# Loading x on the sync queue behind a large weight load, in a decode block on one core

## The chip, the cores and the metric

The kernel runs on one core of one Trainium2 chip. The metric is the device time of one execution in microseconds (us). An execution of one kernel that is over 1.5% above the fastest of the same kernel counts as slow. Times inside a trace are counted from the start of the profiled span, which is some 2 us shorter than the device time.

The engines named below are PE (TensorE, matrix multiplies), DVE (VectorE), ACT (ScalarE) and SP (SyncE, which here does nothing but issue loads). SPq and ACTq are the instruction streams in which SP and ACT issue DMAs (data transfers). The profile counts the work of the core's 16 DMA engines.

## The reference, cut to what matters

One transformer block in decode form: 4 sequences, one token each. A layernorm of x, a projection to 32 query heads, attention over the last 2048 positions of a cache with 4 key/value heads, an output projection with a residual, a second layernorm, and a gated MLP with a residual.

```python
h  = x + attention(layernorm(x) @ wq, k_cache[-2048:], v_cache[-2048:]) @ wo
h2 = h + (silu(layernorm(h) @ w1) * (layernorm(h) @ w3)) @ w2
# x: 4 x 1 x 1024 bf16 (8 KB)     wq: 1024 x 4096 (8 MB)    k, v windows: 8 MB each
# wo: 4096 x 1024 (8 MB)          w1, w3, w2: 7 MB each
```

With four rows of x there is little arithmetic per byte: about 55.6 MB have to be read once. That is the work.

## The kernel before

All large loads go through one on-chip buffer (in SBUF), `ring`, and one queue, the sync queue. A later load reuses the place of an earlier one, so its issue waits until the engines have read what lay there. `load_next(n)` issues the next n entries of a fixed plan.

```python
plan = [
    ("wq", load_rows, (0,         wq_v, N_Q, 0, 4)),     # first half of wq, 4 MB, one DMA
    ("wq", load_rows, (32 * KIB,  wq_v, N_Q, 4, 4)),     # second half, 4 MB, one DMA
    ("k",  load_kv,   (64 * KIB,  A_k_cache, 0)),        # two DMAs of 2 MB
    ("k",  load_kv,   (96 * KIB,  A_k_cache, 2)),        # two DMAs of 2 MB
    ("v",  load_kv,   (128 * KIB, A_v_cache, 0)),
    ("v",  load_kv,   (0,         A_v_cache, 2)),        # takes the place of wq's first half
    ("wo", load_rows, (32 * KIB,  wo_v, D, 0, 32)),
    ("w1", load_rows, (96 * KIB,  w1_v, N_F, 0, 8)),     # takes the place of k and v: waits for OT_ps
    ("w3", ...), ("w3", ...), ("w2", ...), ...           # cut
]

x_sb = act.tile([B, D], BF16)
nc.scalar.dma_start(out=x_sb[:], in_=x_flat)             # x for the layernorm, ScalarE's queue
load_next(5)
# ... cut: ident, eps_t ...
x_q = act.tile([P, CG], BF16)
nc.vector.memset(x_q[:], 0.0)
for j in range(JG):                                      # x again, in the layout of the residual
    nc.scalar.dma_start(out=x_q[QD*j : QD*(j+1) : RS, :], in_=x_flat[:, j*CG : (j+1)*CG])
# ... cut: bn_stats(x_sb), rstd (Sqrt on ScalarE), xn, 8 transposes -> xnT ...
for kc in range(KC):                                     # KC = 8; kc 0..3 read wq's first half
    for hf in range(2):
        for g in range(JG):
            nc.tensor.matmul(q_ps[...], lhsT=xnT[:, kc, :], rhs=loaded["wq"][kc][...], ...)
    if kc == RQ - 1:
        load_next()                                      # second pair of v
# ... cut: q_sb, qt_ps; then 256 transposes of k (kt_ps), scores, softmax, OT_ps = p @ v, y, MLP
```

`x_sb` is needed first of all: without it there is no layernorm and no q. `x_q` is needed only at the residual, at 88 us.

Of the kernel before, what the change touches and what calls it, by code (L numbers as in the profile page):

```python
# [10 lines left out]
P = 128  # L11
# [3 lines left out]
BF16 = mybir.dt.bfloat16  # L15
# [4 lines left out]
def kernel(  # L20
# [13 lines left out]
    nc = tc.nc  # L34
# [14 lines left out]
    x_flat = A_x.flatten_outer_dims()  # L49
# [11 lines left out]
    act = ctx.enter_context(tc.tile_pool(name="act", bufs=1))  # L61
# [3 lines left out]
    JG = 4  # L65
    QD = P // JG
    RS = QD // B
    CQ = Hq * Dh // JG
    CG = D // JG
# [59 lines left out]
    def load_next(n=1):  # L129
        for _ in range(n):  # L130
            if cursor[0] < len(plan):
                kind, f, args = plan[cursor[0]]
                loaded.setdefault(kind, []).extend(f(*args))
                cursor[0] += 1

    x_sb = act.tile([B, D], BF16)
    nc.scalar.dma_start(out=x_sb[:], in_=x_flat)
    load_next(5)

    ident = const.tile([P, P], BF16)  # L140
    make_identity(nc, ident[:])
    eps_t = const.tile([P, 1], FP32)
    nc.vector.memset(eps_t[:], eps)

    x_q = act.tile([P, CG], BF16)
    nc.vector.memset(x_q[:], 0.0)
    for j in range(JG):
        nc.scalar.dma_start(
            out=x_q[QD * j : QD * (j + 1) : RS, :], in_=x_flat[:, j * CG : (j + 1) * CG]
        )  # L150

    psA_cm = tc.tile_pool(name="psA", bufs=1, space=bass.MemoryType.PSUM)
    psA = psA_cm.__enter__()
# [3 lines left out]
    for c in range(2):  # L157
# [8 lines left out]
        out=xn[:], in0=x_sb[:], scalar1=mv[:, 0:1], scalar2=rstd[:, 0:1],  # L166
# [4 lines left out]
    for kc in range(KC):  # L171
# [15 lines left out]
        out=perm[:].rearrange("p (h dq) -> p h dq", dq=JG),  # L187
        in_=ident[:].rearrange("p (dq h) -> p h dq", dq=JG),
# [12 lines left out]
    for j in range(2, JG):  # L201
        nc.vector.tensor_tensor(
            out=same[:, 0, :], in0=same[:, 0, :], in1=ident[:, j * QD : (j + 1) * QD], op=ALU.add
# [24 lines left out]
    for r in range(REP):  # L228
        nc.tensor.transpose(out=qt_ps[:, r, :], in_=q_sb[:, r * Dh : (r + 1) * Dh], identity=ident[:])
    nc.vector.tensor_copy(  # L230
        out=qz[:, :, : Hkv * QD].rearrange("p b (g z) -> p b g z", g=Hkv)[:, :, :, :REP],
        in_=qt_ps[:].rearrange("p r (g x) -> p x g r", g=Hkv)[:, :B, :, :],
# [24 lines left out]
    for u, (b, n) in enumerate(units):  # L257
        k_v = loaded["k"][b]
        kT = ktpool.tile([P, NJ, P], BF16, tag="kT")
        for t in range(NJ // TB):  # L260
            kt_ps = psA.tile([P, TB, P], BF16, tag=f"kt{nt % 4}")
            for jj in range(TB):
                nc.tensor.transpose(  # L263
                    out=kt_ps[:, jj, :], in_=k_v[:, n * NJ + t * TB + jj, :], identity=ident[:]
# [21 lines left out]
        out=Pm[:], in_=scores_ps[:], func=ACT.Exp, bias=nmax[:], scale=1.0, accum_out=rsum[:]  # L286
# [6 lines left out]
    for c in range(NSB):  # L293
# [4 lines left out]
        for g in range(Hkv):  # L298
            if g % 2 == 0:
                nc.vector.tensor_scalar(  # L300
                    out=z[:, :, g, :], in0=pt_ps[:], scalar1=mask[:, g : g + 1], scalar2=None, op0=ALU.mult
# [10 lines left out]
        out=Dm[:], in0=ident[:].rearrange("p (g b r) -> p b g r", g=Hkv, b=B),  # L312
# [38 lines left out]
    for i in range(IO):  # L351
# [34 lines left out]
        out=hn[:], in0=h1[:], scalar1=tot[:, 0:1], scalar2=rstd2[:, 0:1],  # L386
# [5 lines left out]
        out=hnT[:].rearrange("p k x -> p (k x)"), in_=hn[:].rearrange("q (c k) -> q k c", k=KC)  # L392
# [5 lines left out]
    def gate_up(kind, out_ps):  # L398
# [27 lines left out]
        out=hgT[:].rearrange("p i x -> p (i x)"),  # L426
        in_=hg[:].rearrange("q s c -> q (s c)").rearrange("q (c i) -> q i c", i=IF),
# [47 lines left out]
```

## Time and profile before

| | before |
|---|---|
| device time, median of 3 runs | 138.13 us (138.09 to 138.20) |
| bytes moved, mean rate over the span | 55.75 MB, 409 GB/s |
| layernorm starts (first BN_STATS) | 2.52 us |
| first q matmul (needs wq's first half) | 13.05 us |
| second half of the q matmuls (needs wq's second half) | 22.55 us |
| first K transpose | 27.45 us |
| w1's issue on the sync queue (needs OT_ps) | 73.22 us |

From the page of the kernel before: the span, the busy time of the engines, and the DMA row. Each digit of the row is the mean busy share of the 16 DMA engines, in tenths, in one fortieth of the span.

```profile
span 136.3 us, 2302 instructions
...
PE 67.9 (50%) x1035; PEld 42.9 (31%) x1035; DVE 42.6 (31%) x73; ACT 31.0 (23%) x36; POOL 1.7 (1%) x8
...
DMA  5999899999999999997988989989799999989960
```

The DMA engines are busy from the second slice to the last but one. PE, the busiest other engine, works half the time.

The chain of work that ended last, in order of time, for the kernel before (start, length in us, and what the time was spent on):

```profile
1.16 21.35 DMA ring<-in_A_wq_dram
...
22.55 3.18 PE q_ps L215 x32
...
73.22 25.79 DMA ring<-in_B_w_dram
...
101.59 31.37 DMA ring<-in_B_w_dram
```

The two long pieces at the end are waits for loads of the MLP weights. The one of 31.37 us is the last piece of w2, issued at 101.5 us behind transfers that were still queued. A chain that ends in such waits says that the load stream sets the end. The pieces in between (q, and the work on k that is left out here) are on the chain only because w1's issue waits for their results.

The timeline of the kernel before, first 32 us (start, length, engine, line, operation; in brackets the idle time before it and what ended it):

```profile
0.73 0.85 SPq L93 DMA_DIRECT2D ring<-in_A_wq_dram  x2
0.73 0.57 ACTq L137 DMA_DIRECT2D x_sb<-in_A_x_dram  x1
...
1.36 2.55 ACTq L148 DMA_DIRECT2D x_q<-in_A_x_dram  x4
...
2.52 1.27 DVE L158 BATCH_NORM_STATS2 stats<-x_sb 4x6 f32<-4x512 bf16 x2
...
3.94 1.28 ACT L162 ACT_TABLE_LOAD   x1 [3.94 <-DVE stats L158]
...
13.05 3.58 PE L215 MATMUL q_ps<-ring,xnT 128*4 128x512 bf16 x32 [6.05 <-DMA ring<-in_A_wq_dram]
...
22.55 3.15 PE L215 MATMUL q_ps<-ring,xnT 128*4 128x512 bf16 x32 [5.92 <-DMA ring<-in_A_wq_dram]
...
27.45 2.03 PE L263 MATMUL kt_ps<-ident,ring 128*128 128x128 bf16 x33
```

Three things to read here. ScalarE's table load (1.28 us, for the square root) starts only at 3.94 us, because the four x_q issues stand in front of it. The layernorm is ready long before PE can use it: the first q matmul waits 6.05 us more, for wq. And between the two halves of q, PE waits again for wq.

### The profile page before, as it was taken

Reading aid. Unit: us, or ns where it says so; the run is one execution under the profiler, and the core shown is the slowest. Engines: PE = TensorE matmul, PEld = TensorE weight load, DVE = VectorE, ACT = ScalarE, POOL = GpSimd, SP = SyncE. Lnnn points to the kernel's source line nnn. Section 1 sums busy time; section 2 is a strip of 40 time slices with the busy share of each in tenths; the row PEclk is TensorE's granted clock in tenths of the full one; section 3 lists DMA queues with packets and bytes.
Section 4 is the critical chain, followed back from the end, with each engine's and each line's share of the span. In section 5 each row is a group of like instructions: output and inputs, shape, how many; then the busy total and the mean of one; then the engine's idle time right before and its main releaser. Section 6 shows DMA issues by size and latency. Waiting matters only on the chain.

```text
span 136.3 us, 2302 instructions
## 1 busy us (share of the span) xinstructions
PE 67.9 (50%) x1035; PEld 42.9 (31%) x1035; DVE 42.6 (31%) x73; ACT 31.0 (23%) x36; POOL 1.7 (1%) x8
## 2 busy tenths in 40 slices
PE   0101803698989889105259538830096440900960
PEld 0100201274656565001149427610043210300840
DVE  6440000244444444609940030160000695070000
ACT  0400000155555646092944000000003300000001
POOL 5000000000000000000000000000000000000000
PEclk9999999999999999965555865897557777555577
DMA  5999899999999999997988989989799999989960
GB/s 156 462 462 443 385 413 418 423 447 423 428 437 409 437 437 423 435 582 341 538 385 365 524 365 442 459 353 522 328 412 463 434 437 447 429 388 409 426 261 5
DMA packets 2662, 55.75 MB, mean 409 GB/s; under 512 B 312, under 2 KB 344, under 8 KB 604
## 3 DMA queue, kind: packets, MB, share of 16 engines
q1 hardware_dynamic: 2592, 55.58, 95.3%
q8 instruction: 8, 0.13, 0.3%
q10 hardware_dynamic: 60, 0.02, 0.1%
q14 instruction: 2, 0.02, 0.0%
HBM read 55.59 MB, written 0.01 MB: 408 GB/s over the span
## 4 chain that ended last, share of the span: by engine, by line
DMA 58%; PE 21%; ACT 13%; DVE 5%; issue 1%; SPq 0%; ACTq 0%
DMA ring<-in_B_w_dram 42%; DMA ring<-in_A_wq_dram 16%; PE kt_ps L263 9%; ACT kT L269 6%; PE scores_ps L248 5%; ACT z L304 3%; PE q_ps L215 2%; PE g_ps L403 2%; DVE rmax L280 2%; ACT Pm L285 2%; PE OT_ps L326 2%; DVE pT L294 1%; DVE z L300 1%; ACT L285 1%; DVE q_sb L225 1%
## 5 line engine op out<-in xcount | busy, mean ns | idle before, releaser
L269 ACT COPY kT<-kt_ps 128x1024 bf16<-128x1024 bf16 x16 | 15.8, 1014 | 12.0 <-PE kt_ps L263 12.0
L263 PE MATMUL kt_ps<-ident,ring 128*128 128x128 bf16 x256 | 16.4, 219 | 0.0
L263 PEld LDWEIGHTS <-ring 128*128 128x128 bf16 x256 | 14.3, 98 | 5.0 <-issue 4.9
L267 DVE COPY kT<-kt_ps 128x1024 bf16<-128x1024 bf16 x16 | 11.1, 691 | 15.2 <-PE kt_ps L263 15.2
L215 PE MATMUL q_ps<-ring,xnT 128*4 128x512 bf16 x64 | 6.7, 596 | 12.0 <-DMA ring<-in_A_wq_dram 12.0
L403 PEld LDWEIGHTS <-hnT 128*32 128x32 bf16 x128 | 5.3, 137 | 23.1 <-issue 20.5
L248 PE MATMUL scores_ps<-kT,qz 128*32 128x512 bf16 x64 | 9.9, 609 | 3.1 <-ACT kT L269 3.1
L326 PE MATMUL OT_ps<-z,ring 128*128 128x32 bf16 x256 | 7.4, 185 | 6.7 <-ACT z L304 5.0
L403 PE MATMUL u_ps<-ring,hnT 128*32 128x448 bf16 x64 | 6.3, 572 | 8.3 <-DMA ring<-in_B_w_dram 8.3
L403 PE MATMUL g_ps<-ring,hnT 128*32 128x448 bf16 x64 | 5.4, 525 | 9.0 <-DMA ring<-in_B_w_dram 9.0
L433 PE MATMUL y_ps<-ring,hgT 128*32 128x256 bf16 x112 | 5.7, 370 | 8.4 <-DMA ring<-in_B_w_dram 8.3
L326 PEld LDWEIGHTS <-ring 128*128 128x128 bf16 x256 | 7.3, 103 | 7.4 <-issue 7.4
L433 PEld LDWEIGHTS <-hgT 128*32 128x32 bf16 x112 | 4.4, 129 | 10.3 <-issue 6.1
L215 PEld LDWEIGHTS <-xnT 128*4 128x4 bf16 x64 | 2.1, 116 | 16.2 <-issue 15.9
L353 PE MATMUL y_ps<-ring,o 128*32 128x256 bf16 x128 | 5.8, 365 | 2.0 <-DMA ring<-in_A_wo_dram 2.0
L443 ACT CAST res<-y_ps 128x256 bf16<-128x256 f32 x1 | 0.4, 372 | 26.5 <-PE y_ps L433 26.5
L304 ACT ACTIVATE z<-pt_ps,mask 128x512 bf16<-128x512 f32 x8 | 5.3, 687 | 3.5 <-DVE z L300 3.5
L225 DVE TENSOR_SCALAR q_sb<-q_ps 128x512 bf16<-128x512 f32 x1 | 0.7, 690 | 17.2 <-PE q_ps L215 17.2
L353 PEld LDWEIGHTS <-o 128*32 128x32 bf16 x128 | 4.8, 130 | 3.8 <-issue 3.1
L300 DVE TENSOR_SCALAR z<-pt_ps,mask 128x512 bf16<-128x512 f32 x8 | 5.5, 740 | 1.2 <-ACT z L304 0.8
L296 PE MATMUL pt_ps<-pT,perm 128*128 128x512 bf16 x4 | 2.4, 607 | 6.8 <-DVE pT L294 6.8
L417 DVE RECIPROCAL eg<-eg 128x896 f32<-128x896 f32 x1 | 5.8, 5753 | 0.0
(73 smaller groups left out, 40.5 us busy)
## 6 DMA issues: line engine op xcount, KB each, us to landing
ring<-in_A_wq_dram SPq DMA_DIRECT2D x2, 4096.0 KB, 16.8
ring<-in_A_k_cache_dram SPq DMA_DIRECT2D x4, 2048.0 KB, 25.5
ring<-in_A_v_cache_dram SPq DMA_DIRECT2D x4, 2048.0 KB, 40.2
ring<-in_B_w_dram SPq DMA_DIRECT2D x1, 7168.0 KB
ring<-in_B_w_dram SPq DMA_DIRECT2D x2, 3584.0 KB, 28.6
ring<-in_B_w_dram SPq DMA_DIRECT2D x1, 4352.0 KB
ring<-in_B_w_dram SPq DMA_DIRECT2D x1, 1792.0 KB
ring<-in_B_w_dram SPq DMA_DIRECT2D x1, 768.0 KB
```

What stands on the lines that cost most here:

```text
L215: nc.tensor.matmul(q_ps[QD * g : QD * g + B, hf * 512 : (hf + 1) * 512], lhsT=xnT[:, kc, :], rhs=wq_t[:, c0 : c0 + 512], start=(kc == 0), ...
L248: nc.tensor.matmul(scores_ps[QD * g : QD * (g + 1), n * 512 : (n + 1) * 512], lhsT=qz[:, b, g * QD : (g + 1) * QD], rhs=kT_v[:, g, :, :], ...
L263: nc.tensor.transpose(out=kt_ps[:, jj, :], in_=k_v[:, n * NJ + t * TB + jj, :], identity=ident[:])
L267: nc.vector.tensor_copy(out=kT[:, t * TB : (t + 1) * TB, :], in_=kt_ps[:])
L269: nc.scalar.copy(out=kT[:, t * TB : (t + 1) * TB, :], in_=kt_ps[:])
L300: nc.vector.tensor_scalar(out=z[:, :, g, :], in0=pt_ps[:], scalar1=mask[:, g : g + 1], scalar2=None, op0=ALU.mult)
L304: nc.scalar.mul(out=z[:, :, g, :], in_=pt_ps[:], mul=mask[:, g : g + 1])
L326: nc.tensor.matmul(OT_ps[:, b, :], lhsT=loaded["v"][b][:, j, :], rhs=PTz[j // NJ][:, (j % NJ) * B + b, :, :], start=(j == 0), stop=(j == J ...
L353: nc.tensor.matmul(y_ps[QD * j : QD * (j + 1), :], lhsT=o4[:, i, :, :].rearrange("p b s -> p (b s)"), rhs=loaded["wo"][i][:, j * CG : (j + ...
L403: nc.tensor.matmul(out_ps[QD * j : QD * (j + 1), hf, :HF], lhsT=hnT[:, k, :], rhs=loaded[kind][k][:, c0 : c0 + HF], start=(k == 0), stop=( ...
L417: nc.vector.reciprocal(out=eg[:], in_=eg[:])
L433: nc.tensor.matmul(y2_ps[QD * j : QD * (j + 1), :], lhsT=hgT[:, i, :], rhs=loaded["w2"][i][:, j * CG : (j + 1) * CG], start=False, stop=(i ...
```

## The change

The intent was to take all loads of x off ScalarE's queue. `x_sb` goes on the sync queue behind wq's first half, `x_q` behind its second half.

```diff
     x_sb = act.tile([B, D], BF16)
-    nc.scalar.dma_start(out=x_sb[:], in_=x_flat)
-    load_next(5)
+    x_q = act.tile([P, CG], BF16)
+    nc.vector.memset(x_q[:], 0.0)
+    load_next()
+    nc.sync.dma_start(out=x_sb[:], in_=x_flat)
+    load_next()
+    for j in range(JG):
+        nc.sync.dma_start(
+            out=x_q[QD * j : QD * (j + 1) : RS, :], in_=x_flat[:, j * CG : (j + 1) * CG]
+        )
+    load_next(3)
 
     ident = const.tile([P, P], BF16)
 ...
-    x_q = act.tile([P, CG], BF16)
-    nc.vector.memset(x_q[:], 0.0)
-    for j in range(JG):
-        nc.scalar.dma_start(
-            out=x_q[QD * j : QD * (j + 1) : RS, :], in_=x_flat[:, j * CG : (j + 1) * CG]
-        )
```

## The prediction

> **What bounds the kernel now.** The load stream. The page gives 55.75 MB at a mean 409 GB/s; the DMA row of the 40 slices is near 9 from the second slice to the last but one. The chain that ended last is 58% DMA; its last long link is a 31.4 us DMA wait (101.6 to 133.0 us) on w2, issued behind transfers still queued. PE is 50% busy, DVE 31%, ACT 23%. So a change counts only if it (a) starves the stream, (b) adds engine time to it, or (c) delays compute so far that a buffer release reaches the sync queue late.
>
> **What the change moves.** Bytes and arithmetic stay. x (5 small loads, 16 KB together) leaves ScalarE's queue; x_sb goes behind wq's first 4 MB on the sync queue, x_q behind its second.
>
> 1. x_sb lands with wq's first half, not at about 2.2 us. The Trainium skill, "DMA: Bandwidth & Descriptors", section "Queues, rings and completion order", says that an engine consumes a ring's descriptors in order and alternates between rings packet by packet; no run shows it here yet. In the timeline the first BN_STATS starts at 2.52 us and the first q matmul, which waits for wq's first half, at 13.05. I expect BN_STATS at 12.6 to 13.3 us.
>
> 2. The layernorm chain is exposed behind that landing. In the timeline, BN_STATS to first q matmul weights took 4.74 us, of which about 1.1 us was ScalarE's table load (1.28 us), held up by the four x_q issues (2.55 us) before it. Those leave ScalarE, so the table loads early. Chain: about 3.6 us; first q matmul at about 16.6 us.
>
> 3. The first 32 q matmuls take 3.58 us: done at about 20.2 us. The second half of wq is usable only at 22.55 us. About 2.3 us of slack remain, so q_ps, q_sb and the first K transposes (27.54 us) stay put. The 3.5 us delay is paid inside a wait.
>
> 4. Sync queue: five more issues at about 0.6 us each, 3 us, while wq's 8 MB keep the engines busy until 22 us. Completion semaphores shift with the order of issue: the instruction orders show that the second k load now waits for wq's first half (before: for x_sb), the fourth for wq's second half. At about 22.5 us, 6 MB of k, some 14 us of stream, are still queued, so nothing starves. The v and wo loads wait for the same things as before; w1's issue at 73.2 us hangs on OT_ps.
>
> 5. Engine time of x is the same tiny packets on another queue.
>
> **On the critical path:** nothing, by this count.
>
> **Predicted time:** 138.1 us (138.13 before), range 137.6 to 138.8. Chances: faster by over 2% 0.01, within 2% 0.97, slower by over 2% 0.02.
>
> **What the profile would show.** Right: BN_STATS at about 13 us, ScalarE's table load within the first 3 us, first q matmul at 16 to 17 us, second half of q at 22.3 to 22.9 us, first K transposes near 27.5 us, k load issues stretching to about 22.5 us, ScalarE's queue with 20 packets instead of 60, the same DMA tail. Wrong step 1: BN_STATS near 2.5 us, or well after 13.3. Wrong step 3: the second half of q waits for PE's own first half, not for DMA. Wrong step 4: a dip in the DMA slices between 22 and 42 us.
>
> **What would make it wrong.** x_sb landing over 2 us after wq's first half; small packets stalling the big ones behind them in one ring (then wq's second half lands late and the tail shifts by as much, perhaps 1 us); the first use of ScalarE's queue for the output adding to the tail; or moved k issues changing which engines lag at the end.

## The result, and the profile after

The kernel after takes 138.20 us (median of 6 runs, 138.15 to 138.25), the kernel before 138.14 us (6 runs of the same rounds, 138.09 to 138.20). The ratio is 1.0004, with a 95% interval of 0.9991 to 1.0017: no difference. A ratio here is the mean time of one kernel's fast runs over the mean of the other's fast runs of the same rounds, so it isn't quite the ratio of the medians.

The same lines of the page, after:

```profile
span 136.5 us, 2302 instructions
...
PE 68.4 (50%) x1035; PEld 42.7 (31%) x1035; DVE 42.5 (31%) x73; ACT 31.0 (23%) x36; POOL 1.7 (1%) x8
...
DMA  5999899999999999998988989989799999989960
```

The timeline of the kernel after, first 32 us:

```profile
0.73 1.28 ACT L163 ACT_TABLE_LOAD   x1 [0.73 <-PEq L460]
...
0.73 0.38 SPq L93 DMA_DIRECT2D ring<-in_A_wq_dram  x1
...
1.18 0.35 SPq L140 DMA_DIRECT2D x_sb<-in_A_x_dram  x1
...
1.98 2.59 SPq L143 DMA_DIRECT2D x_q<-in_A_x_dram  x4
...
4.61 18.44 SPq L101 DMA_DIRECT2D ring<-in_A_k_cache_dram  x4
12.93 1.27 DVE L159 BATCH_NORM_STATS2 stats<-x_sb 4x6 f32<-4x512 bf16 x2 [8.88 <-DMA x_sb<-in_A_x_dram]
...
16.49 3.25 PE L216 MATMUL q_ps<-ring,xnT 128*4 128x512 bf16 x32 [0.27 <-DVE xnT L175]
...
22.54 3.48 PE L216 MATMUL q_ps<-ring,xnT 128*4 128x512 bf16 x32 [2.79 <-DMA ring<-in_A_wq_dram]
...
27.67 2.10 PE L264 MATMUL kt_ps<-ident,ring 128*128 128x128 bf16 x33
```

Much has moved. BN_STATS starts at 12.93 us instead of 2.52, after DVE had idled 8.88 us for x_sb. The table load runs at 0.73 us, long before it is needed, so the chain from BN_STATS to the first q matmul takes 16.49 - 12.93 = 3.56 us instead of 4.74. The first half of q starts 3.44 us later than before and ends at 16.49 + 3.25 = 19.74 us. Then PE waits 2.79 us for wq's second half, and that half starts at 22.54 us, as before (22.55). The delay of more than 3 us was paid out of a wait that had been 5.92 us long.

The chain of waits, after:

```profile
1.58 20.92 DMA ring<-in_A_wq_dram
...
22.54 3.50 PE q_ps L216 x32
...
73.52 25.67 DMA ring<-in_B_w_dram
...
101.77 31.28 DMA ring<-in_B_w_dram
```

The q part of the chain is 0.3 us longer. The second half of q took 3.48 us instead of 3.15, and the same half took between 3.15 and 3.58 us in the traces, also where x came early. w1's issue comes 0.30 us later (73.52 us). The wait behind it is shorter by 0.12 us, and the last long wait ends at 101.77 + 31.28 = 133.05 us instead of 101.59 + 31.37 = 132.96. The packet records of the two traces say the same of the whole stream: each further 4 MB of it has arrived at the same time in both, within 0.1 us.

Two smaller facts. The DMA queue view counts 20 packets on ScalarE's queue instead of 60. The issue of the output on ScalarE took 1.13 us instead of 0.61 (see the last sections).

### The profile page after: what moved, and what is told of

It reads as the page before. It is cut to its first block, busy times and chain, and to the rows that moved or that the text cites. A ratio compares the mean times of both kernels' runs of the same rounds, so it can differ in the third digit from the quotient of the medians.

```text
span 136.5 us, 2302 instructions
## 1 busy us (share of the span) xinstructions
PE 68.4 (50%) x1035; PEld 42.7 (31%) x1035; DVE 42.5 (31%) x73; ACT 31.0 (23%) x36; POOL 1.7 (1%) x8
## 4 chain that ended last, share of the span: by engine, by line
DMA 57%; PE 21%; ACT 13%; DVE 5%; issue 1%; SPq 1%; ACTq 0%
DMA ring<-in_B_w_dram 42%; DMA ring<-in_A_wq_dram 15%; PE kt_ps L264 9%; ACT kT L270 6%; PE scores_ps L249 5%; ACT z L305 3%; PE q_ps L216 3%; PE g_ps L404 2%; DVE rmax L281 2%; ACT Pm L286 2%; PE OT_ps L327 1%; DVE pT L295 1%; DVE z L301 1%; ACT L286 1%; DVE q_sb L226 1%
## 5 line engine op out<-in xcount | busy, mean ns | idle before, releaser
L434 PE MATMUL y_ps<-ring,hgT 128*32 128x256 bf16 x112 | 6.2, 391 | 7.9 <-DMA ring<-in_B_w_dram 7.8
L173 PE MATMUL tp_ps<-ident,xn 4*128 4x4 bf16 x8 | 0.7, 199 | 15.6 <-DVE xn L166 15.6
L173 PEld LDWEIGHTS <-xn 4*128 4x128 bf16 x8 | 0.6, 160 | 15.6 <-DVE xn L166 15.6
L354 PEld LDWEIGHTS <-o 128*32 128x32 bf16 x128 | 4.2, 127 | 3.1 <-DVE o L343 1.9
## 6 DMA issues: line engine op xcount, KB each, us to landing
ring<-in_B_w_dram SPq DMA_DIRECT2D x2, 3584.0 KB, 29.8
```

What stands on the lines that cost most here:

```text
L354: nc.tensor.matmul(y_ps[QD * j : QD * (j + 1), :], lhsT=o4[:, i, :, :].rearrange("p b s -> p (b s)"), rhs=loaded["wo"][i][:, j * CG : (j + ...
L434: nc.tensor.matmul(y2_ps[QD * j : QD * (j + 1), :], lhsT=hgT[:, i, :], rhs=loaded["w2"][i][:, j * CG : (j + 1) * CG], start=False, stop=(i ...
```

## The experiments

The theory, called S in the expectations: the load stream sets the time. x's delay is paid inside PE's wait for wq, and even a later q would cost nothing as long as w1 is issued before the stream runs dry. The rivals: C, two effects cancelled (the later q costs, the freed ScalarE queue pays); Q, the time follows the start of the work on k, which the change left in place by luck.

All kernels gave correct results. Both halves alone, all of x in front of wq, and x behind wq (its first six runs) ran on one chip with 11 runs of the kernel before (median 138.14 us). `x_sb` alone in front, the repeat of x behind wq, and the two later places ran on another (11 runs, median 138.20 us).

### One half of the change at a time

Only `x_sb` moves, and the four x_q loads stay on ScalarE's queue (diff against the kernel after):

```diff
-        nc.sync.dma_start(
+        nc.scalar.dma_start(
             out=x_q[QD * j : QD * (j + 1) : RS, :], in_=x_flat[:, j * CG : (j + 1) * CG]
```

> Only x_sb moves behind wq's first half; the four x_q loads stay on ScalarE's queue. Theory S (the load stream sets the time, and x_sb's delay is paid inside the wait for wq's second half): 138.0 to 138.4 us, ratio within 0.3% of 1; BN_STATS at about 12.9 us; ScalarE's table load held back again to about 3.4 us by the x_q issues but still long before BN_STATS; second half of q at about 22.5 us. Rival C (two effects cancelled: the later q costs, the freed ScalarE queue pays): this run has only the cost, 139 to 141.5 us. Rival Q (time follows the start of the K transposes): same as S here, as that start hardly moved.

Measured: 138.27 us (5 runs, 138.14 to 138.32), ratio 1.0004 (0.9991 to 1.0017). Its timeline:

```profile
1.03 3.04 ACTq L143 DMA_DIRECT2D x_q<-in_A_x_dram  x4
...
4.09 1.28 ACT L162 ACT_TABLE_LOAD   x1 [4.09 <-DVE same L205]
13.37 1.27 DVE L158 BATCH_NORM_STATS2 stats<-x_sb 4x6 f32<-4x512 bf16 x2 [9.32 <-DMA x_sb<-in_A_x_dram]
```

Only `x_q` moves, and `x_sb` stays first on ScalarE's queue:

```diff
-    load_next()
-    nc.sync.dma_start(out=x_sb[:], in_=x_flat)
+    nc.scalar.dma_start(out=x_sb[:], in_=x_flat)
+    load_next()
     load_next()
```

> Only the four x_q loads move to the sync queue; x_sb stays first on ScalarE's queue. Theory S: 138.0 to 138.3 us; BN_STATS at about 2.5 us, first q matmul still at about 13.0 us (it waits for wq), table load early so that the layernorm chain ends about 1.1 us sooner, for nothing. Rival C: this run has only the gain, 135 to 137.5 us. Rival Q: same as S.

Measured: 138.24 us (5 runs, 138.15 to 138.66), ratio 1.0010 (0.9998 to 1.0022). Its timeline:

```profile
1.33 1.28 ACT L162 ACT_TABLE_LOAD   x1 [1.33 <-PEq L459]
...
2.59 1.27 DVE L158 BATCH_NORM_STATS2 stats<-x_sb 4x6 f32<-4x512 bf16 x2
...
12.97 3.33 PE L215 MATMUL q_ps<-ring,xnT 128*4 128x512 bf16 x32 [7.08 <-DMA ring<-in_A_wq_dram]
```

Each half alone is worth nothing. In the first, x is as late as in the kernel after and the table load is held back again to 4.09 us (expected: about 3.4; the x_q issues took 3.04 us). BN_STATS came at 13.37 us, about 0.5 later than expected (why is open: by the packet records x_sb's last packet ended at 12.41 us, in the kernel after at 12.37). It costs nothing. In the second, the freed ScalarE queue is all there is: the table load comes at 1.33 us instead of 3.94, and PE still starts q at 12.97 us, because wq isn't there before. It gains nothing. Two effects that cancel would have shown as a loss in one run and a gain in the other. C falls.

### x in front of wq

If the stream sets the time, what may not be delayed is its start. All five x loads in front of wq, on the sync queue:

```diff
-    load_next()
     nc.sync.dma_start(out=x_sb[:], in_=x_flat)
-    load_next()
     for j in range(JG):
         nc.sync.dma_start(out=x_q[...], in_=x_flat[...])
-    load_next(3)
+    load_next(5)
```

> All five x loads on the sync queue IN FRONT of wq: wq's first issue goes from 0.73 us to about 3.7 us (0.4 + 4 x 0.65 us of issue). Theory S: the stream starts 3.0 us later and the whole time grows by as much, 140.8 to 141.5 us (2.0 to 2.4% slower), every later landing shifted alike. If the stream had slack of its own: 138.1 to 139 us.

Measured: 141.48 us (4 runs, 141.22 to 141.79), ratio 1.024 (1.0226 to 1.0255). Timeline:

```profile
0.73 0.36 SPq L139 DMA_DIRECT2D x_sb<-in_A_x_dram  x1
...
1.16 2.58 SPq L141 DMA_DIRECT2D x_q<-in_A_x_dram  x4
...
3.78 0.91 SPq L93 DMA_DIRECT2D ring<-in_A_wq_dram  x2
...
16.09 3.58 PE L213 MATMUL q_ps<-ring,xnT 128*4 128x512 bf16 x32 [10.48 <-DMA ring<-in_A_wq_dram]
...
25.77 3.58 PE L213 MATMUL q_ps<-ring,xnT 128*4 128x512 bf16 x32 [6.10 <-DMA ring<-in_A_wq_dram]
```

wq's first issue moved from 0.73 to 3.78 us, by 3.05 us. In 138.14 us, 2.4% are 3.3 us, so the late start was paid about in full. A rival is that the loss came later: w1's issue was late too, at 78.11 us. The packet records rule it out. The stream was 3.05 to 3.15 us behind that of the kernel before from its first 4 MB to its end, and w1's first packets followed wo's last (83.2 to 84.9 us) without a gap. Here x came earlier than before (BN_STATS at 2.38 us), and this is one of the two slowest kernels. In this queue the early place is worth more to wq than to x.

A smaller dose, `x_sb` alone in front and `x_q` behind wq:

```diff
-    load_next()
     nc.sync.dma_start(out=x_sb[:], in_=x_flat)
-    load_next()
+    load_next(2)
     for j in range(JG):   # x_q, as in the kernel after
```

> Only x_sb's load goes in front of wq on the sync queue (one issue of about 0.4 us); x_q stays behind wq. Theory S: the stream starts 0.4 us later and the time grows by that alone, 138.4 to 138.8 us (+0.3 to +0.6 over before); the first q matmul, waiting for wq, at about 13.4 us. If the loss of the run with all x loads in front came from the four small x_q loads on the stream and not from the late start: no change, 138.0 to 138.3.

Measured: 138.54 us (5 runs, 138.50 to 138.81), ratio 1.0028 (1.0015 to 1.0040), which is 0.4 us of 138.2. Its timeline:

```profile
1.16 0.84 SPq L93 DMA_DIRECT2D ring<-in_A_wq_dram  x2
...
13.18 3.58 PE L214 MATMUL q_ps<-ring,xnT 128*4 128x512 bf16 x32 [7.58 <-DMA ring<-in_A_wq_dram]
```

wq's issue came at 1.16 us, 0.43 later than before. One small issue ahead of the stream costs its own issue time, five cost five. The first q matmul came at 13.18 us (expected: about 13.4).

### x later and later

The other way round: how late may x come? `x_sb` behind both halves of wq:

```diff
-    load_next()
+    load_next(2)
     nc.sync.dma_start(out=x_sb[:], in_=x_flat)
-    load_next()
     for j in range(JG):   # x_q, as in the kernel after
```

> x_sb behind BOTH halves of wq: it lands at about 22.3 us, the layernorm chain takes 3.6 us, the 64 q matmuls 6.7 us, so q ends at about 33 us instead of 25.7 and everything up to OT_ps moves by about 7.2 us; w1's issue goes from 73.2 to about 80.4 us. Before, wo's last completions come at 79.9 to 81.8 us, so theory S expects the stream to be just short of running dry: 138.0 to 139.0 us (0 to +0.9). Rival Q (time follows the start of the K transposes): +7, about 145 us. Rival C: +5 or more.

Measured: of 6 runs four were fast, at 138.05 to 138.80 us, and two slow, at 140.17 and 140.25. The ratio of the fast runs is 1.0013 (0.9995 to 1.0030). The same kernel again:

> The same kernel as e3_behind_wq again, because its profile fell in the slow state. Theory S: fast runs at 138.0 to 138.9 us; w1's issue at about 78 us, a gap of up to about 1.5 us on some DMA engines at about 81 us, and the last w2 piece within 0.8 us of before. If the K delay cost time directly: fast runs at 142 us or more, which the first run already speaks against.

Measured: 138.29, 138.38, 138.48 and 139.96 us, ratio 1.0041 (1.0002 to 1.0079). The profiled run is the one of 138.38 us:

```profile
22.57 1.27 DVE L157 BATCH_NORM_STATS2 stats<-x_sb 4x6 f32<-4x512 bf16 x2 [18.51 <-DMA x_sb<-in_A_x_dram]
...
26.13 5.75 PE L214 MATMUL q_ps<-ring,xnT 128*4 128x512 bf16 x64 [0.27 <-DVE xnT L173]
```

BN_STATS starts at 22.57 us in it, and the second half of q has no wait left to hide in: all 64 q matmuls run in one piece, from 26.13 to 31.88 us. And still the time is, in most runs, that of before. What happened to w1's issue, in the sync queue's timeline:

```profile
77.14 11.70 SPq L93 DMA_DIRECT2D ring<-in_B_w_dram  x3
```

It came at 77.14 us, 3.9 us later than before, although q ended some 6 us later. Part of the delay was won back: in this kernel's instruction order 55 transposes of k, instead of 33, stand between the last q matmul and the first score, and from the end of q to the end of the scores it takes 27.6 us instead of 29.8. (So the expectation of 80.4 us was too late. It had assumed that everything up to OT_ps would move by the same 7.2 us.) The slow runs of this kernel, and the one of 139.96 us, have no explanation here; the kernel before showed none in the 11 runs beside each. In the one slow run that has a trace (140.17 us), w1's issue came at 77.96 us, the stream was some 0.5 us behind from there on, and the last DMA engine ended w2 1.0 us after all the others.

The next dose, behind wq and the first of the four k loads (done by a hook in `load_kv`, which issues x_sb after its first DMA), and then behind both loads of the first k pair:

```diff
+    load_next(2)                                          # wq
+    hook.append(lambda: nc.sync.dma_start(out=x_sb[:], in_=x_flat))
+    load_next(1)                                          # k load 0, x_sb, k load 1
     for j in range(JG):   # x_q
         ...
+    load_next(2)
```

> x_sb behind wq AND the first k load: it lands about 4.9 us later than behind wq alone (27.2 us). In e3 w1's issue came at 77.96 us; here I expect 82.8 us, its first packets about 1 us later, at 83.8, while wo's last completions stay at 79.9 to 81.8. Theory S: the stream runs dry for about 2 to 4 us before w1 and the time grows by the gap of the slowest engine, +1.5 to +3.0 us: 139.6 to 141.2. Rival Q (time follows the K phase): +9.5, about 147.6. If the stream never runs dry: 138.1.

```diff
+    load_next(3)                                          # wq, both k loads of the first pair
     nc.sync.dma_start(out=x_sb[:], in_=x_flat)
     for j in range(JG):   # x_q
         ...
+    load_next(2)
```

> x_sb behind wq and BOTH loads of k's first pair: it lands another 4.9 us later, about 32 us; w1's issue at about 87.6 us. Theory S: past the point where the stream runs dry every further microsecond is paid in full, so about 4.8 us more than e5: 144.0 to 146.2 us (+6 to +8). The slope from e5 to e6 should be 1 (4.3 to 5.3 us); a slope near 0 would refute S. Rival Q: +14, about 152.

Measured: 140.16 us (4 runs, 140.05 to 140.28), ratio 1.0141 (1.0128 to 1.0154), and 145.18 us (6 runs, 144.60 to 146.39), ratio 1.0508 (1.0474 to 1.0541). x's arrival, in the first and then in the second of these kernels:

```profile
27.43 1.27 DVE L162 BATCH_NORM_STATS2 stats<-x_sb 4x6 f32<-4x512 bf16 x2 [23.38 <-DMA x_sb<-in_A_x_dram]
```

```profile
32.22 1.27 DVE L157 BATCH_NORM_STATS2 stats<-x_sb 4x6 f32<-4x512 bf16 x2 [28.17 <-DMA x_sb<-in_A_x_dram]
```

The issue of w1 in the sync queue's timeline, in the first and then in the second of these kernels:

```profile
80.23 9.01 SPq L93 DMA_DIRECT2D ring<-in_B_w_dram  x3
```

```profile
84.41 4.04 SPq L93 DMA_DIRECT2D ring<-in_B_w_dram  x2
```

The two times lie in the expected ranges, but w1's issue came 2.6 and 3.2 us earlier than expected (82.8 and 87.6 us). So the way from x to w1 was judged too long, and the cost of a gap too small, and that both times came out right is in part luck.

Does the stream run dry where w1 comes late? The windows view shows it (stretch in us, its length, busy time of the engines, granted PE clock, DMA share, GB/s). The kernel before:

```profile
core 0: us, PE busy (x) PEld busy (x) DVE busy (x) ACT busy (x) POOL busy (x), PEclk, DMA share, GB/s
...
76.00:92.00 16.00, 8.65 (x188) 6.89 (x188) 4.09 (x14) 0.29 (x1) 0.00 (x0) 0.78 0.96 411
92.00:130.00 38.00, 15.45 (x196) 8.41 (x197) 10.53 (x6) 2.20 (x2) 0.00 (x0) 0.61 0.99 426
```

x behind wq:

```profile
76.00:92.00 16.00, 11.52 (x333) 9.59 (x329) 2.38 (x7) 0.91 (x1) 0.00 (x0) 0.61 0.97 417
```

x behind wq and the first k load:

```profile
76.00:92.00 16.00, 12.08 (x366) 10.58 (x367) 2.50 (x5) 2.88 (x4) 0.00 (x0) 0.69 0.90 371
```

x behind wq and the first pair of k:

```profile
76.00:92.00 16.00, 10.16 (x296) 8.92 (x299) 6.30 (x12) 6.13 (x10) 0.00 (x0) 0.61 0.63 256
92.00:130.00 38.00, 16.29 (x232) 8.62 (x225) 13.30 (x16) 2.49 (x3) 0.00 (x0) 0.68 1.00 429
```

From 76 to 92 us the rate is 411 GB/s before, 417 with x behind wq, then 371 and 256. Against 411 over 16 us the last two lack 0.64 and 2.48 MB, and at 425 GB/s these are 1.5 and 5.8 us of stream. The two profiled runs, at 140.07 and 144.62 us, are 1.9 and 6.5 us longer than the profiled run of before (138.12). So the dry stretch holds most of the loss. The packet records show part of the rest at the end: the first DMA engine to finish w2 does so 1.7 and 5.7 us later than before, the last one 1.9 and 6.4 us later. Why the engines end less evenly was not tested, and what is left in the third kernel, some 0.2 us, isn't located. From 92 to 130 us the four move 426, 421, 425 and 429 GB/s: once w1 runs, nothing is different. The packet records of the traces say the same: the last packets of wo end between 79.7 and 81.8 us in all four; w1's first packets follow them without a gap before and with x behind wq, start at 81.2 to 81.9 us in the third kernel, and at 85.4 to 86.1 us in the fourth. After such a gap the first packets of w1 are slow as well: on average 2.7 us each instead of 2.1. Ahead of w1, from 5 to 79 us, the engines were never idle in any of the four, so x_q's place and the later issues of k and v, which these kernels change too, starved nothing.

The whole row of doses, with the kernels in order of x's arrival:

| x_sb stands | BN_STATS starts | w1's issue | device time, median |
|---|---|---|---|
| first on ScalarE's queue (before) | 2.52 us | 73.22 us | 138.14 us |
| behind half of wq (after) | 12.93 us | 73.52 us | 138.20 us |
| behind wq | 22.57 us | 77.14 us | 138.43 us |
| behind wq and the first k load | 27.43 us | 80.23 us | 140.16 us |
| behind wq and the first pair of k | 32.22 us | 84.41 us | 145.18 us |

The last three ran on the second chip, where the kernel before had 138.20 us. The first 20 us of delay cost nearly nothing, and the last 4.79 us cost 5.0 by the medians (4.55 between the two profiled runs). In the two last traces, w1's first packet started 0.96 and 0.97 us after its issue. The first DMA engine is done with wo at about 79.9 us, so an issue up to about 78.9 us would be soon enough. That is an estimate, worked out from these packet times, and an upper one: in the slow run with a trace, an issue at 77.96 us went with 0.5 us of lost stream (one slow run, so no more than a hint). At 77.14 us none was lost, so the kernel after, at 73.52 us, has at least 3.6 us to spare. Q falls with this: the work on k began 4.4 us later in the third line without a loss of that size, and in the last two lines the K transposes start at 27.31 and 27.28 us, no later than before, and the time grows.

No experiment gave a version that beats the two kernels. Everything that moved the time made it longer, and the two limits that it ran into, the start of the stream and the bytes, are the same in both. (No run changed the bytes.)

## Why the prediction was right

- **What bounds the kernel.** Right, and shown from both ends: a later start of the stream was paid in full (0.43 us of later issue for 0.4 us, 3.05 for 3.3), and a gap inside it too (fourth and fifth line of the table).
- **Step 1, x_sb lands with wq's first half.** Right: 12.93 us against 12.6 to 13.3. The trace agrees with what the Trainium skill, "DMA: Bandwidth & Descriptors", section "Queues, rings and completion order", says of the order within a ring: 8 KB waited about 10 us behind 4 MB. It shows the alternation too: in the kernel before, the first packets of x_q on ScalarE's queue (data and completion in turn) come at 6.04, 7.27 and 8.49 us, each one wq packet of 1.2 us after the last. Each further load in front of it moved BN_STATS on by that load's time: 9.6 us for 4 MB, and 4.9 and 4.8 us for 2 MB each.
- **Step 2, the chain of the layernorm.** Right: 3.56 us against about 3.6, and the table load at 0.73 us. The Trainium skill, "ScalarE: Activation LUTs", section "What ACT_TABLE_LOAD costs", gives about 1283 ns for it, and the trace has 1.28 us.
- **Step 3, the delay is paid inside a wait.** Right in kind, and a little cautious in size: 2.79 us were left over instead of 2.3, because the first half of q took 3.25 us instead of 3.58. What the prediction didn't say is that this wait was not the last reserve. With x behind all of wq it was used up, and the time still hardly moved. The larger reserve lies at w1's issue, which step 4 names without saying how much room it has.
- **Step 4, the sync queue doesn't starve.** Right: the five issues took 0.35 + 2.59 = 2.94 us, the k issues stretched to 4.61 + 18.44 = 23.05 us, and the DMA row stays at 9 there. That the shifted waits of the k loads are harmless was read from this row, and the packet records agree (the stream of the two kernels is the same within 0.1 us). No run tested it apart.
- **Step 5 and the critical path.** Right within what can be measured: the ratio is 1.0004.
- **A listed risk that came up.** The output's issue on ScalarE's queue did get longer, 1.13 us for 0.61. By the packet records the first output packet came 1.29 us after the issue began, before 1.25. So it cost at most a few hundredths.

## What to carry to other kernels

In a kernel that is bound by one load stream, ask of a moved small load two things only: does it delay the first large load, and does it delay the issue that the stream will next depend on? Between these two an operand can come 10 us later for nothing, as here; and an operand that is loaded first, on the stream's own queue, costs its issue time in full. Find the reserve by moving the operand later step by step until the time rises, for the chain that ended last names the waits but not how much room each has.

## What the Trainium skill lacked or had wrong

- "DMA: Bandwidth & Descriptors", section "Issuing engines are not separate DMA queues": it says that issuing from several engines "will only save the time on the sequencer". Here the choice of the queue also decided when a small load arrives. x_q, on ScalarE's queue beside wq, had its data packets between 6.0 and 12.5 us, and on the sync queue behind wq between 21.8 and 22.2 us. (For x_sb, 2.52 and 12.93 us, the early place counts as well: on the sync queue in front of wq, BN_STATS came at 2.38 us.) This section doesn't say it; it follows from the rings in the section named in step 1.
- The same page, section "Where 436 GB/s comes from": it says that for transfers from HBM a limit of about 358 GB/s per core binds. The kernel before, on one core, moved 409 GB/s over its whole span and 426 GB/s from 92 to 130 us. The page's own measurement of one core alone (425 GB/s) fits. The page gives about 358 GB/s there for two cores of one HBM domain that stream at once; without this condition the sentence doesn't hold.
- None of the pages that were read has the following: the issue of the output's DMA on ScalarE took 0.61 to 0.63 us in the three kernels in which ScalarE's queue had carried loads of x, and 1.13 to 1.14 us in the six kernels (seven traces, counting the repeat) in which it had carried none, with hardly any effect on when the packets started. The cause is open.
